# Every second column as the loaded operand of an FFN's products, at chosen distances in SBUF (attention and squared-ReLU FFN in float32, one core)

## The chip, the core and the metric

The kernel runs on one core of a Trainium2 chip. The metric is the device time of one execution in microseconds. A core has a matrix engine (TensorE, PE in the profile), which holds a loaded operand of up to 128 x 128 (LDWEIGHTS, PEld) and streams the columns of a moving operand past it (MATMUL); VectorE (DVE), ScalarE (ACT) and GpSimd (POOL), which work on 128 partitions side by side; and SyncE (SP), whose queue issues the DMAs. SBUF is the working memory, one row of bytes per partition; PSUM takes the products.

## The reference

Eight batches of eight heads, 576 positions, head dimension 64. Each head's output is a sum of two attentions: one on positions averaged by fours and repeated, one on a band of seven positions. Its 4608 tokens of 512 values then go through an FFN:

```python
x = np.ascontiguousarray(attn_out.transpose(0, 2, 1, 3)).reshape(B * S, H * D)
h = x @ w_in                      # 4608 x 512 by 512 x 2048
g = s * (np.maximum(h, 0.0) ** 2) + b
return g @ w_out                  # 2048 x 512
```

## The kernel before

**The FFN.** Tokens go in 18 tiles of 256 (index t), the 2048 columns of w_in in eight pairs of 128 (index p, so one p is 256 columns of w_in and 256 rows of w_out). Each operand is kept as a high and a low part in a rounded format (float32r), and a product is three matmuls: high by high, high by low, low by high. `gemm1(t, p)` forms h transposed: for each of the two column tiles j of the pair and each of four parts k of the 512 values, a 128 x 128 piece of `wi[p]` is the loaded operand and 256 tokens of `xh` or `xl` are the moving one (L544 to L546, 24 matmuls of 256 columns). ACT squares the result, ACT and DVE split it into `gh` and `gl` (or into one tile `gb` for every third p). `gemm2(t, p)` has 128 tokens of `gh` or `gl` as the loaded operand and 512 columns of `wo[p]` as the moving one (L589 to L591, 12 matmuls of 512 columns), and sums over p in PSUM. At p=7 the sum is scaled, the bias is added (L601), and the tile goes out. A step is one `gemm1` and a `gemm2` of some steps before.

**Order.** The list `order` gives the steps: the first three token tiles are mixed over p, then t by t. `advance` lets attention's generators run between steps to a target, so their matmuls and element-wise work stand among the FFN's. Within that, the framework places instructions by its own simulation of time.

**Memory.** All tiles come from three pools: `cst` (constants), `one` (one buffer for each tag) and `two` (two buffers for each tag). They are laid behind one another in the order in which tags are first asked for, so a tile asked for early moves all that come later. `xh` and `xl` of the token tiles other than t=2 have two buffers each, `gh` and `gl` two each, `wi` and `wo` one for each p. For t=2 the tags "os" and "xl2" are borrowed.

In both kernels the five engines' queues hold the same instructions in the same order. What differs is steps and places. Where the operands start, in bytes modulo 256:

```
                              before              after
wi, loaded, p = 2 3 4 5       96                  192
wi, loaded, p = 6             96                  64
wi, loaded, p = 7 0 1         224                 64
xh and xl, moving             32, 32 (2 buffers)  128, 192 (2 buffers)
xh and xl of t=2, moving      96                  192
gh and gl, loaded             32, 32 (2 buffers)  64, 128 (2 buffers)
gb, loaded                    96                  192
wo, moving, p = 2 3 4 5       96                  192
wo, moving, p = 6             96                  64
wo, moving, p = 7 0 1         224                 64
```

Pieces within a tile start at multiples of 512 bytes before; after, the second f tile of a pair starts 4 bytes behind the first.

Of the kernel before, what the change touches and what calls it, by code (L numbers as in the profile page):

```python
# [54 lines left out]

W_MAX = (1.875 - 2.0 ** -23) * 2.0 ** (31 - 127)

OB = {0: (0, 1), 1: (2, 3), 2: (6, 7)}


@with_exitstack
def attention_ffn_kernel(ctx, tc, qk, vw_in, vr_in, vdm, qkn, vn, w_in, w_out, s_in, b_in, out):
# [22 lines left out]

    room = {}

    def make_room(i):
        sc, dg = flat(f"wi{6 - i}", 2048), flat(f"wo{6 - i}", 2048)
        if i == 1:  # L90
            big = flat("x", HP * S, two)
            lp = {"vw": take(big, 0, [P, NG, P]), "vd": take(big, 768, [KM, FAC, P])}
            pl, at = big, 1280
        else:
            big = flat("wi2" if i == 2 else "wo2", 2048)
            pl, at = flat("os" if i == 2 else "xl2", 1024), 512
            lp = {"qk": take(big, 0, [P, 2, SP]), "vw": take(big, 2 * SP, [P, NG, P]),
                  "vd": take(pl, 0, [KM, FAC, P])}
        lp["vr"] = take(sc, 1792, [P, FAC, D])
        return {"sc": sc, "dg": dg, "load": lp, "pl": take(pl, at, [P, 2 * NG, 32]),  # L100
                "sm": take(pl, at + 384, [P, 2, 2 * NG])}
# [26 lines left out]

    mask = cst.tile([P, 3, 32], F32, name="mask")
    nc.gpsimd.memset(mask, 0.0)

    def keep(ap, pattern, base, cm):
# [56 lines left out]
    wi, wo, wst = {}, {}, {}  # L191

    src_i = w_in.bitcast(I32).rearrange("(k c) f -> c k f", c=P)
    src_o = w_out.bitcast(I32).rearrange("(j f) c -> f j c", f=P)

    def load_w(p):

        parts = (("i", src_i[:, :, 512 * p : 512 * p + 512]), ("o", src_o[:, 2 * p : 2 * p + 2]))
        for op, src in parts:
            st = one.tile([P, 1024, 2], I32, tag=f"w{op}{STAGE[p]}", name="wst")  # L200
            nc.sync.dma_start(st.rearrange("p (k f) t -> p k (f t)", k=src.shape[1]), src)
            wst[(p, op)] = st

    def load_quarter(p, op, i):
        if op == "i":
            src = src_i[:, i, 512 * p : 512 * p + 512]
        else:
            src = src_o[:, 2 * p + i // 2, 512 * (i % 2) : 512 * (i % 2) + 512]
        st = two.tile([P, 256, 2], I32, tag="pv", name="wst")
        nc.sync.dma_start(st.rearrange("p f t -> p (f t)"), src)  # L210
        return st
# [21 lines left out]
            nc.vector.tensor_tensor(lo[:, js], f[:, js], hi.bitcast(F32)[:, js], ALU.subtract)  # L233

    def split_w(p):
        with tc.high_priority(offset=-BEHIND.get(p, 0)):
            split_parts(p)

    def split_parts(p):
        wi[p] = one.tile([P, 2, NK, 256], F32R, tag=f"wi{p}", name="wi")  # L240
        wo[p] = one.tile([P, 2, 2, DM], F32R, tag=f"wo{p}", name="wo")
        for op, w in (("i", wi[p]), ("o", wo[p])):
            fl = w.rearrange("p s k f -> p s (k f)")
            if p < len(STAGE):
                st = wst.pop((p, op))
                for j in range(0, 1024, CHUNK[p]):
                    js = slice(j, j + CHUNK[p])
                    convert(st[:, js], fl[:, 0, js], fl[:, 1, js], op, p)
            else:
                for i in range(4):  # L250
                    cs = slice(256 * i, 256 * i + 256)
                    convert(load_quarter(p, op, i), fl[:, 0, cs], fl[:, 1, cs], op, p)
# [80 lines left out]
    def first_unit(b, hp, banks):  # L333
# [71 lines left out]
        try:  # L405
            next(dn)
        except StopIteration as e:
            up = e.value
        ups = tmp([P, SD], "ups")
        nc.scalar.copy(ups, up)  # L410
        yield
        for f in range(2):
# [28 lines left out]
    def local_unit(b, g, banks):  # L441
# [4 lines left out]
        for h in range(2):  # L446
            lqk = one.tile([P, 2 * CH + 2 * HALO, D], F32, tag="big", name="lqk")
            nc.sync.dma_start(lqk, qkn[GROUPS.index((b, g)), h])
            lv = one.tile([P, CH + 2 * HALO, D], F32, tag="vw", name="lv")
            nc.sync.dma_start(lv, vn[GROUPS.index((b, g)), h])  # L450
            ls = take(st[:, h], 0, [P, CH, NO])
            sums = st[:, h, 64 : 64 + CH]
            for o in range(NO):
                pr = two.tile([P, CH, D], F32, tag="pl", name="pr")
                nc.gpsimd.tensor_tensor(  # L455
                    pr, lqk[:, 0:CH], lqk[:, CH + o : 2 * CH + o], ALU.mult)
                nc.vector.tensor_reduce(ls[:, :, o], pr, AX.X, ALU.add)  # L457
                yield
            row = lambda t: t.unsqueeze(2).to_broadcast([P, CH, NO])
            nc.vector.tensor_tensor(ls, ls, omask, ALU.add)  # L460
            lr = two.tile([P, 2, CH], F32, tag="lr", name="lr")
            nc.vector.tensor_reduce(lr[:, 0], ls, AX.X, ALU.max)
            nc.vector.tensor_tensor(ls, ls, row(lr[:, 0]), ALU.subtract)
            nc.scalar.activation(ls, ls, AF.Exp, scale=SCALE)
            nc.vector.tensor_reduce(sums, ls, AX.X, ALU.add)
            nc.vector.tensor_scalar(sums, sums, 1e-9, None, ALU.add)
            nc.vector.reciprocal(lr[:, 1], sums)
            nc.vector.tensor_tensor(ls, ls, row(lr[:, 1]), ALU.mult)
            yield
            for o in range(NO):  # L470
                w = ls[:, :, o : o + 1].to_broadcast([P, CH, D])
                if o == 0:
                    nc.vector.tensor_tensor(acc[:, :, h], lv[:, 0:CH], w, ALU.mult)
                else:
                    pv = two.tile([P, CH, D], F32, tag="pv", name="pv")
                    nc.vector.tensor_tensor(pv, lv[:, o : o + CH], w, ALU.mult)  # L476
                    (nc.vector if o % 3 == 1 else nc.gpsimd).tensor_tensor(  # L477
                        acc[:, :, h], acc[:, :, h], pv, ALU.add)
                yield
# [35 lines left out]
    xs = {}  # L515

    def split_x(t):
        tags = ("os", "xl2") if t == 2 else ("xh", "xl")
        pool = one if t == 2 else two
        xh = pool.tile([P, HP, TB], F32R, tag=tags[0], name="xh")  # L520
        xl = pool.tile([P, HP, TB], F32R, tag=tags[1], name="xl")
        t0 = t * TB
        while t0 < (t + 1) * TB:
            b = t0 // S
            while (b, HP - 1) not in complete:
                next(gen)
            n = min((t + 1) * TB, (b + 1) * S) - t0
            src = xt[b][:, :, t0 - b * S : t0 - b * S + n]
            dst = slice(t0 - t * TB, t0 - t * TB + n)
            nc.scalar.copy(xh[:, :, dst], src)  # L530
            nc.vector.tensor_tensor(
                xl[:, :, dst], src, xh[:, :, dst].bitcast(F32), ALU.subtract)
            t0 += n
        xs[t] = (xh, xl)

    gt = {}
    oacc = {}

    def gemm1(t, p):
        xh, xl = xs[t]  # L540
        ph = bank(6 if t >= 3 and p % 2 else 7 if t == 1 and p < HF else 4, [P, 2, TB], "ph")
        for j, k in itertools.product(range(2), range(NK)):
            f = slice(P * j, P * j + P)
            nc.tensor.matmul(ph[:, j], wi[p][:, 0, k, f], xh[:, k], start=(k == 0), stop=False)  # L544
            nc.tensor.matmul(ph[:, j], wi[p][:, 0, k, f], xl[:, k], start=False, stop=False)  # L545
            nc.tensor.matmul(ph[:, j], wi[p][:, 1, k, f], xh[:, k], start=False, stop=(k == NK - 1))  # L546
# [1 line left out]
            both = one.tile([P, 2, 2, TB], F32R, tag="xl2", name="gb")  # L548
            gh, gl = both[:, 0], both[:, 1]
        else:  # L550
            gh = two.tile([P, 2, TB], F32R, tag="gh", name="gh")
            gl = two.tile([P, 2, TB], F32R, tag="gl", name="gl")
        with tc.high_priority():
            nc.scalar.activation(ph, ph, AF.Relu)  # L554
            nc.scalar.activation(ph, ph, AF.Square)  # L555
# [18 lines left out]
    def gemm2(t, p):  # L574
# [5 lines left out]
            oacc[t] = [bank(i, [P, DM], "po") for i in ob]  # L580
        po = oacc[t]
        end = t == NB - 1 and p == NFP - 1
        os_ = one.tile([P, 2, DM], F32, tag="os", name="os") if p == NFP - 1 else None
        for m in range(2):
            ms = slice(P * m, P * m + P)
            for j in range(2):
                first = p == 0 and j == 0
                last = p == NFP - 1 and j == 1
# [1 line left out]
                nc.tensor.matmul(po[m], gh[:, j, ms], wo[p][:, 1, j], start=False, stop=False)  # L590
                nc.tensor.matmul(po[m], gl[:, j, ms], wo[p][:, 0, j], start=False, stop=last)  # L591
            if end:
                r0 = TB * t + P * m
                for c in (0, DM // 2):
                    cs = slice(c, c + DM // 2)
                    nc.vector.scalar_tensor_tensor(
                        os_[:, m, cs], po[m][:, cs], sb_s, bias[:, cs], ALU.mult, ALU.add)
                    nc.sync.dma_start(out[r0 : r0 + P, cs], os_[:, m, cs])
        if p == NFP - 1 and not end:
            for m in range(2):  # L600
                nc.vector.scalar_tensor_tensor(  # L601
                    os_[:, m], po[m], sb_s, bias, ALU.mult, ALU.add)
            nc.sync.dma_start(
                out[TB * t : TB * t + TB, :].rearrange("(m p) c -> p m c", p=P), os_)


    units = [(b, hp) for b in range(B) for hp in range(HP)]
# [10 lines left out]
    for hp in range(2, HP):  # L618
        load_pair(0, hp)
    load_w(0)  # L620
    sb_s = cst.tile([P, 1], F32, name="sb_s")
    nc.sync.dma_start(sb_s, bass.AP(s_in.tensor, s_in.offset, [[0, P], [1, 1]]))
    sb_b = cst.tile([P, 1], F32, name="sb_b")
    nc.sync.dma_start(sb_b, bass.AP(b_in.tensor, b_in.offset, [[0, P], [1, 1]]))
    clear(1)
    bk = banks(0, 1, 2, 3, 5, 6, 7)
# [7 lines left out]
    split_w(0)  # L634
    load_w(1)
    load_w(2)
    split_x(0)
    split_x(1)


# [117 lines left out]
```

## Time and profile before

| | |
|---|---|
| time, median of 3 runs | 975.49 us (lowest 974.06) |
| profiled execution: time, span | 974.94 us, 973.1 us |
| TensorE busy | 937.4 us, 96% of the span |
| VectorE, ScalarE, GpSimd busy | 646.8, 478.8, 425.0 us |
| mean granted TensorE clock | 0.982 |

The span is from the first to the last instruction. A line such as `L544 PE MATMUL ph<-xh,wi 128*128 128x256 f32` is line 544's matmul on TensorE into the tile ph from xh (moving) and wi (loaded), 128 rows by 128 loaded columns, 256 moving columns. Matmuls overlap one another, so a busy time is not a rate; the distance from one start to the next is.

### The profile page before, as it was taken

The page shows a single profiled execution, that of the slowest core. Times are in us where ns is not written, and L with a number is a line of the kernel's source. Part 1 is how long each engine was busy: PE and PEld are TensorE (multiplying, and loading weights), DVE is VectorE, ACT ScalarE, POOL GpSimd, SP SyncE. Part 2 cuts the span into 40 slices and gives each one's busy share as a digit, 9 for nine tenths or more (in the row PEclk, how much of TensorE's full clock was granted, in tenths as well). Part 3 has the DMA queues.
Part 4 walks back from the last instruction along what each step waited for, and adds up shares of the span by engine and source line. Part 5 has one row for each costly group of instructions (what it writes and reads, how often), then busy time and mean ns, then how long its engine had stood idle before and what let it go on. Part 6 is the DMA issues. An engine that isn't in the chain of part 4 may idle for free.

```text
span 973.1 us, 18535 instructions
## 1 busy us (share of the span) xinstructions
PE 937.4 (96%) x7316; PEld 840.0 (86%) x7316; DVE 646.8 (66%) x1175; ACT 478.8 (49%) x1141; POOL 425.0 (44%) x455
## 2 busy tenths in 40 slices
PE   5769999999999999999999999999999999999998
PEld 4558888788999989889989898999899999998997
DVE  5999985864468778878787975876787772211121
ACT  5878775453755454534545344454454444333231
POOL 9422011100167686776767585575776750000000
PEclk9579999999999999999999999999999999999999
DMA  9746422102233232322323232231323100000000
GB/s 314 261 132 204 166 65 73 60 31 86 88 122 112 86 101 85 133 65 72 106 93 102 80 98 80 78 112 58 112 90 111 55 23 1 23 1 22 1 23 22
DMA packets 32103, 86.26 MB, mean 89 GB/s; under 512 B 3344, under 2 KB 7952, under 8 KB 32016
## 3 DMA queue, kind: packets, MB, share of 16 engines
q1 hardware_dynamic: 32016, 85.08, 26.4%
q8 instruction: 57, 0.93, 0.4%
q14 instruction: 30, 0.25, 0.1%
HBM read 75.63 MB, written 9.44 MB: 87 GB/s over the span
## 4 chain that ended last, share of the span: by engine, by line
PE 76%; DVE 7%; POOL 6%; DMA 6%; issue 3%; ACT 2%; DVEq 0%; SPq 0%; POOLq 0%; ACTq 0%
PE ph L544 12%; PE ph L545 12%; PE ph L546 12%; PE po L589 11%; PE po L590 11%; PE po L591 11%; DMA tqk<-in_qk_dram 3%; POOL pr L455 2%; PE sa L297 2%; DMA lqk<-in_qkn_dram 1%; POOL acc L477 1%; DMA wst<-in_moe_w_out_dram 1%; PE up L328 1%; PE ol L420 1%; PE ot L486 1%
## 5 line engine op out<-in xcount | busy, mean ns | idle before, releaser
L544 PE MATMUL ph<-xh,wi 128*128 128x256 f32 x1152 | 327.2, 284 | 5.3 <-DVE gl L557 2.5
L545 PE MATMUL ph<-xl,wi 128*128 128x256 f32 x1152 | 324.0, 281 | 0.0
L546 PE MATMUL ph<-xh,wi 128*128 128x256 f32 x1152 | 323.6, 281 | 0.0
L455 POOL TENSOR_TENSOR pr<-lqk 128x576 f32<-128x576 f32 x140 | 203.0, 1473 | 90.1 <-DMA lqk<-in_qkn_dram 53.9
L544 PEld LDWEIGHTS ph<-xh,wi 128*128 128x128 f32 x1152 | 217.1, 188 | 12.8 <-DVE gl L557 3.4
L545 PEld LDWEIGHTS ph<-xl,wi 128*128 128x128 f32 x1152 | 217.0, 188 | 5.0 <-issue 0.2
L546 PEld LDWEIGHTS ph<-xh,wi 128*128 128x128 f32 x1152 | 217.3, 189 | 0.1
L554 ACT ACTIVATE ph<-ph 128x512 f32<-128x512 f32 x144 | 83.7, 581 | 236.7 <-PE ph L546 236.5
L589 PE MATMUL po<-wo,gh 128*128 128x512 f32 x456 | 183.0, 402 | 0.2 <-ACT gh L556 0.2
L590 PE MATMUL po<-wo,gh 128*128 128x512 f32 x456 | 181.5, 398 | 0.0
L591 PE MATMUL po<-wo,gl 128*128 128x512 f32 x456 | 179.5, 399 | 0.0
L557 DVE TENSOR_TENSOR gl<-ph,gh 128x512 fp32r<-128x512 f32 x114 | 77.9, 683 | 110.9 <-ACT gh L556 110.5
L477 POOL TENSOR_TENSOR acc<-acc,pv 128x576 f32<-128x576 f32 x80 | 114.6, 1433 | 68.0 <-DVE acc L477 33.5
L457 DVE TENSOR_REDUCE st<-pr 128x9 f32<-128x576 f32 x140 | 105.9, 756 | 40.9 <-POOL pr L455 38.8
L287 POOL TENSOR_TENSOR dq<-vq 64x64 f32<-64x64 f32 x58 | 25.6, 441 | 192.4 <-PE up L326 190.2
L556 ACT CAST gh<-ph 128x512 fp32r<-128x512 f32 x114 | 66.8, 586 | 70.6 <-PE po L590 68.5
L591 PEld LDWEIGHTS po<-wo,gl 128*128 128x128 f32 x456 | 85.7, 188 | 17.3 <-issue 0.2
L476 DVE TENSOR_TENSOR pv<-lv,st 128x576 f32<-128x576 f32 x120 | 87.2, 747 | 20.2 <-POOL acc L477 19.6
L589 PEld LDWEIGHTS po<-wo,gh 128*128 128x128 f32 x456 | 85.7, 188 | 15.8 <-ACT gh L556 0.8
L590 PEld LDWEIGHTS po<-wo,gh 128*128 128x128 f32 x456 | 85.8, 188 | 15.6
L555 ACT ACTIVATE ph<-ph 128x512 f32<-128x512 f32 x144 | 83.8, 582 | 3.4
L590 PE MATMUL po<-wo,gb 128*128 128x512 f32 x120 | 48.2, 402 | 0.0
(145 smaller groups left out, 1261.1 us busy)
## 6 DMA issues: line engine op xcount, KB each, us to landing
tqk<-in_qk_dram SPq DMA_DIRECT2D x30, 584.0 KB, 4.0
lqk<-in_qkn_dram SPq DMA_DIRECT2D x20, 768.0 KB, 4.4
lv<-in_vn_dram SPq DMA_DIRECT2D x20, 480.0 KB, 3.5
out_dram<-os SPq DMA_DIRECT2D x17, 512.0 KB, 3.0
wst<-in_moe_w_in_dram SPq DMA_DIRECT2D x7, 1024.0 KB, 5.5
wst<-in_moe_w_out_dram SPq DMA_DIRECT2D x7, 1024.0 KB, 5.3
tvd<-in_vdm_dram SPq DMA_DIRECT2D x29, 160.0 KB, 2.7
tvr<-in_vr_dram SPq DMA_DIRECT2D x29, 128.0 KB, 2.1
```

Source lines behind the costliest of these rows:

```text
L455: nc.gpsimd.tensor_tensor(pr, lqk[:, 0:CH], lqk[:, CH + o : 2 * CH + o], ALU.mult)
L457: nc.vector.tensor_reduce(ls[:, :, o], pr, AX.X, ALU.add)
L476: nc.vector.tensor_tensor(pv, lv[:, o : o + CH], w, ALU.mult)
L477: (nc.vector if o % 3 == 1 else nc.gpsimd).tensor_tensor(acc[:, :, h], acc[:, :, h], pv, ALU.add)
L544: nc.tensor.matmul(ph[:, j], wi[p][:, 0, k, f], xh[:, k], start=(k == 0), stop=False)
L545: nc.tensor.matmul(ph[:, j], wi[p][:, 0, k, f], xl[:, k], start=False, stop=False)
L546: nc.tensor.matmul(ph[:, j], wi[p][:, 1, k, f], xh[:, k], start=False, stop=(k == NK - 1))
L554: nc.scalar.activation(ph, ph, AF.Relu)
L555: nc.scalar.activation(ph, ph, AF.Square)
L589: nc.tensor.matmul(po[m], gh[:, j, ms], wo[p][:, 0, j], start=first, stop=False)
L590: nc.tensor.matmul(po[m], gh[:, j, ms], wo[p][:, 1, j], start=False, stop=False)
L591: nc.tensor.matmul(po[m], gl[:, j, ms], wo[p][:, 0, j], start=False, stop=last)
```

## The change

The loaded operand of both products becomes every second column of the same memory: in `gemm1` the two f tiles of a pair are its even and its odd columns, in `gemm2` the two token tiles are the even and the odd tokens. So that the products stay the same, w_out's rows are loaded in the same alternation, and the output's rows are written so. Empty tiles (`skip`) of 128, 192 and 64 bytes and 16 unused elements at the end of each x buffer set where operands start. To make room and to set the start of all, the mask takes a buffer of the tag "pv", `ups` that of `ptm`, `sb_s` and `sb_b` one tile, and `xh` and `xl` lie in one tile.

```diff
+SKIP = (0, 128, 192, 0, 0, 0, 64, 0, 0)
...
+    def skip(n, pool=one):
+        if n:
+            pool.tile([P, n // 4], F32, tag=f"skip{next(skips)}", name="skip")
...
-    mask = cst.tile([P, 3, 32], F32, name="mask")
+    mask = two.tile([P, 3, 32], F32, tag="pv", name="mask")
...
-    src_o = w_out.bitcast(I32).rearrange("(j f) c -> f j c", f=P)
+    src_o = w_out.bitcast(I32).rearrange("(q f j) c -> f q j c", f=P, j=2)
...
+        if p == 0:
+            skip(SKIP[1])
...
     def split_w(p):
+        if p == 0:
+            skip(SKIP[2])
...
     def split_parts(p):
+        if p == 1:
+            for h in range(2):
+                one.tile([P, 2, CH], F32, tag=f"lr{h}", name="lr")
+            skip(SKIP[-1])
...
-        ups = tmp([P, SD], "ups")
+        ups = tmp([P, SD], "ups") if alt else one.tile([P, SD], F32, tag="ptm", name="ups")
...
-            lr = two.tile([P, 2, CH], F32, tag="lr", name="lr")
+            lr = one.tile([P, 2, CH], F32, tag=f"lr{h}", name="lr")
...
-        xh = pool.tile([P, HP, TB], F32R, tag=tags[0], name="xh")
-        xl = pool.tile([P, HP, TB], F32R, tag=tags[1], name="xl")
+        if t == 2:
+            xh, xl = (pool.tile([P, HP * TB], F32R, tag=g, name="x2") for g in tags)
+        else:
+            both = pool.tile([P, 2 * HP * TB + 16], F32R, tag="xhl", name="xhl")
+            xh, xl = both[:, 0 : HP * TB], both[:, HP * TB : 2 * HP * TB]
+        xh, xl = (v.rearrange("p (k c) -> p k c", k=HP) for v in (xh, xl))
...
-            f = slice(P * j, P * j + P)
+            f = slice(j, 256, 2)
...
-            gh = two.tile([P, 2, TB], F32R, tag="gh", name="gh")
-            gl = two.tile([P, 2, TB], F32R, tag="gl", name="gl")
+            i = next(gs)
+            if i < 2:
+                skip(SKIP[4 + 2 * i])
+            gh = one.tile([P, 2, TB], F32R, tag=f"gh{i % 2}", name="gh")
+            if i < 2:
+                skip(SKIP[5 + 2 * i])
+            gl = one.tile([P, 2, TB], F32R, tag=f"gl{i % 2}", name="gl")
...
+        rows = out[TB * t : TB * t + TB, :].rearrange("(p m) c -> p m c", m=2)
...
-            ms = slice(P * m, P * m + P)
+            ms = slice(m, TB, 2)
...
-                    nc.sync.dma_start(out[r0 : r0 + P, cs], os_[:, m, cs])
+                    nc.sync.dma_start(rows[:, m, cs], os_[:, m, cs])
...
-    sb_s = cst.tile([P, 1], F32, name="sb_s")
+    sb = cst.tile([P, 2], F32, name="sb")
+    sb_s, sb_b = sb[:, 0:1], sb[:, 1:2]
```

More of the change, by code (lines that the diff above doesn't have):

```diff
@@ L86, in attention_ffn_kernel @@
     room = {}
+    def skip(n, pool=one):
+        if n:
+            pool.tile([P, n // 4], F32, tag=f"skip{next(skips)}", name="skip")
+    skips = itertools.count()
     def make_room(i):
+        if i == 1:
+            skip(SKIP[0])
         sc, dg = flat(f"wi{6 - i}", 2048), flat(f"wo{6 - i}", 2048)
@@ L193, in attention_ffn_kernel @@
     src_i = w_in.bitcast(I32).rearrange("(k c) f -> c k f", c=P)
-    src_o = w_out.bitcast(I32).rearrange("(j f) c -> f j c", f=P)
+    src_o = w_out.bitcast(I32).rearrange("(q f j) c -> f q j c", f=P, j=2)
     def load_w(p):
-        parts = (("i", src_i[:, :, 512 * p : 512 * p + 512]), ("o", src_o[:, 2 * p : 2 * p + 2]))
+        parts = (("i", src_i[:, :, 512 * p : 512 * p + 512]), ("o", src_o[:, p]))
+        if p == 0:
+            skip(SKIP[1])
         for op, src in parts:
@@ L207, in load_quarter @@
         else:
-            src = src_o[:, 2 * p + i // 2, 512 * (i % 2) : 512 * (i % 2) + 512]
+            src = src_o[:, p, i // 2, 512 * (i % 2) : 512 * (i % 2) + 512]
         st = two.tile([P, 256, 2], I32, tag="pv", name="wst")
@@ L517, in split_x @@
     def split_x(t):
-        tags = ("os", "xl2") if t == 2 else ("xh", "xl")
+        tags = ("os", "xl2")
         pool = one if t == 2 else two
-        xh = pool.tile([P, HP, TB], F32R, tag=tags[0], name="xh")
-        xl = pool.tile([P, HP, TB], F32R, tag=tags[1], name="xl")
+        if t == 2:
[4 more added lines that the diff above has]
+        xh, xl = (v.rearrange("p (k c) -> p k c", k=HP) for v in (xh, xl))
         t0 = t * TB
@@ L536, in attention_ffn_kernel @@
     gt = {}
+    gs = itertools.count()
     oacc = {}
@@ L592, in gemm2 @@
             if end:
-                r0 = TB * t + P * m
                 for c in (0, DM // 2):
@@ L602, in gemm2 @@
                     os_[:, m], po[m], sb_s, bias, ALU.mult, ALU.add)
-            nc.sync.dma_start(
-                out[TB * t : TB * t + TB, :].rearrange("(m p) c -> p m c", p=P), os_)
+            nc.sync.dma_start(rows, os_)
     units = [(b, hp) for b in range(B) for hp in range(HP)]
@@ L620, in attention_ffn_kernel @@
     load_w(0)
-    sb_s = cst.tile([P, 1], F32, name="sb_s")
+    sb = cst.tile([P, 2], F32, name="sb")
+    sb_s, sb_b = sb[:, 0:1], sb[:, 1:2]
     nc.sync.dma_start(sb_s, bass.AP(s_in.tensor, s_in.offset, [[0, P], [1, 1]]))
-    sb_b = cst.tile([P, 1], F32, name="sb_b")
     nc.sync.dma_start(sb_b, bass.AP(b_in.tensor, b_in.offset, [[0, P], [1, 1]]))
@@ L636, in attention_ffn_kernel @@
     load_w(2)
+    skip(SKIP[3], two)
     split_x(0)
```

## The prediction

> **What bounds the kernel now.** I read the shares of the engines first, then the stretches of time, then who TensorE waited for, and last the starts of single matmuls. The page:
>
> ```profile
> PE 937.4 (96%) x7316; PEld 840.0 (86%) x7316; DVE 646.8 (66%) x1175; ACT 478.8 (49%) x1141; POOL 425.0 (44%) x455
> PE 76%; DVE 7%; POOL 6%; DMA 6%; issue 3%; ACT 2%; DVEq 0%; SPq 0%; POOLq 0%; ACTq 0%
> ```
>
> By stretches (us, then each engine's busy time and count, the granted TensorE clock, the DMA share, GB/s):
>
> ```profile
> 20.00:60.00 40.00, 27.23 (x441) 22.20 (x441) 35.83 (x87) 33.05 (x96) 18.02 (x27) 0.70 0.69 237
> 60.00:100.00 40.00, 35.75 (x365) 32.10 (x364) 39.56 (x71) 32.00 (x62) 7.50 (x10) 0.87 0.56 188
> 100.00:970.00 870.00, 864.51 (x6298) 777.61 (x6297) 559.12 (x995) 405.13 (x957) 381.52 (x368) 1.00 0.22 72
> 820.00:920.00 100.00, 100.00 (x650) 90.75 (x649) 17.72 (x24) 33.26 (x57) 0.00 (x0) 1.00 0.03 11
> ```
>
> From 100 to 970 us TensorE is busy for 864.5 of 870 us at a granted clock of 1.00. Behind 820 us nobody else has much to do and it is still full. So the kernel is TensorE's stream of matmuls, and the time is their number times the distance from one start to the next. The longest waits of TensorE are few and early (us in total, times, longest):
>
> ```profile
> PE sa L297 <- ACT dq L277: 7.3, 1, 7.3
> PE ol L420 <- ACT db L403: 4.6, 2, 2.7
> PE ph L544 <- DVE gl L557: 2.5, 3, 1.2
> ```
>
> A busy time hides the distance, since matmuls overlap. It has to be read from starts (start us, duration us). One step of the FFN is 24 matmuls of 256 columns (L544 to L546) and 12 of 512 (L589 to L591). First the first product at two f pairs p, then the second product at two places:
>
> ```profile
> 886.12 0.28 PE L544 MATMUL ph<-xh,wi 128*128 128x256 f32 x1
> 886.36 0.28 PE L546 MATMUL ph<-xh,wi 128*128 128x256 f32 x1
> ...
> 888.74 0.28 PE L546 MATMUL ph<-xh,wi 128*128 128x256 f32 x1
> ...
> 866.58 0.28 PE L544 MATMUL ph<-xh,wi 128*128 128x256 f32 x1
> ...
> 869.29 0.28 PE L546 MATMUL ph<-xh,wi 128*128 128x256 f32 x1
> ...
> 517.26 0.39 PE L589 MATMUL po<-wo,gb 128*128 128x512 f32 x1
> ...
> 519.30 0.28 PE L544 MATMUL ph<-xh,wi 128*128 128x256 f32 x1
> ...
> 495.60 0.39 PE L591 MATMUL po<-wo,gl 128*128 128x512 f32 x1
> ...
> 496.30 0.40 PE L591 MATMUL po<-wo,gl 128*128 128x512 f32 x1
> ```
>
> The same instruction runs at two speeds. At p=2 (886 us) the last 22 of a group of 24 start (888.74 - 886.36) / 21 = **113.3 ns** apart. At p=7 (866 us) a group of 24 takes (869.29 - 866.58) / 23 = **117.8 ns** each. In the second product nine distances from 517.26 to 519.30 give **226.7 ns**, and three from 495.60 to 496.30 give 233 ns. In the late part every group at p = 2 to 5 is of the fast kind and every one at p = 6, 7, 0, 1 of the slow kind, for one token tile after another, while clock and instruction stay the same. Only the tiles' places in SBUF differ by p. At t=2, where x stands elsewhere, it is slower still, (209.80 - 207.04) / 23 = **120.0 ns**:
>
> ```profile
> 207.04 0.28 PE L544 MATMUL ph<-xh,wi 128*128 128x256 f32 x1
> ...
> 209.80 0.28 PE L546 MATMUL ph<-xh,wi 128*128 128x256 f32 x1
> ```
>
> So something that hangs on addresses costs up to 4.5 or 6.7 ns a matmul. It is this that a change of steps and distances can touch.
>
> **What the change touches.** The five queues hold the same instructions in the same order as before; only names, steps, addresses and the semaphores of three waits differ. So nothing is counted anew. The terms are rates.
>
> How much there is to gain follows from one token tile, that is eight steps:
>
> ```profile
> 841.72 0.28 PE L544 MATMUL ph<-xh,wi 128*128 128x256 f32 x1
> ...
> 886.12 0.28 PE L544 MATMUL ph<-xh,wi 128*128 128x256 f32 x1
> ...
> 930.52 0.28 PE L544 MATMUL ph<-xh,wi 128*128 128x256 f32 x1
> ```
>
> From p=2 to p=2 it is 44.40 us, twice. With all its matmuls at the fast rows it would be 8 x (24 x 113.3 + 12 x 226.7) ns = 43.51 us. The address-dependent part is 0.89 us, times 18 token tiles **16.0 us**. Earlier tiles have more of it (t=2), and stretches in which attention's matmuls stand between have waits that stay; I leave both out.
>
> What the stride does to a load: no loaded operand of this kernel has a step now, so its price is bounded by rows. Loads of 32, 64, 96 and 128 columns from 120 us on (mean ns):
>
> ```profile
> L377 PEld LDWEIGHTS sl<-tqk 64*32 64x32 f32 x480 | 5.6, 107 | 2.4 <-issue 1.3
> L420 PEld LDWEIGHTS ol<-db,tvw 128*64 128x64 f32 x144 | 6.3, 136 | 2.2 <-issue 1.3 <-ACT ups L410 0.4
> L297 PEld LDWEIGHTS sa<-kd,dq 128*96 128x96 f32 x150 | 21.6, 162 | 3.4
> L545 PEld LDWEIGHTS ph<-xl,wi 128*128 128x128 f32 x1080 | 203.2, 188 | 4.4
> 886.37 0.19 PEld L544 LDWEIGHTS ph<-xh,wi 128*128 128x128 f32 x1
> ```
>
> That is (188 - 107) / 96 = 0.84 ns a column, so a load reads for about 108 ns behind a fixed 80 ns. It starts 10 ns or less behind the matmul before (886.37 against 886.36) and runs beside that matmul's columns. From this follow two things. In 108 ns a load with step one passes 512 bytes of its row, while 256 moving columns pass 1024 bytes in 113.3 ns: the moving operand overtakes the load. With step two the load passes 1024 bytes too. The two then run **in step**, and how far apart they are stays as the addresses set it, which is what the distances in memory would be good for. Second, in the first product 108 of 113.3 ns are filled by the load, so a load that reads over 5% slower becomes the bound there; in the second product (226.7) it could double for nothing. Lower end: the whole 16.0 us go. Upper end: loads at double price, 216 ns, put (216 - 116) x 3456 matmuls = 346 us on top. I take the lower one, since the load has as many columns as before and the kernel's rows price columns alone.
>
> [...] No run here has shown a stepped load yet.
>
> The rest I cost at nothing. The mask lies in one of the two "pv" buffers; the next user of it stands behind the mask's last reader (L149, 0.4 us) on DVE anyway. "ups" shares a buffer with "ptm": the next copy L319 on ACT must now find L423 done, which is two 0.45 us operations of DVE, nine times, 8 us of ACT if nothing hid it; ACT is busy 405 of 870 us and TensorE has other matmuls queued. "gh", "gl", "lr" and "xh" with "xl" keep two buffers each. The w_out loads and the outputs move the same bytes in longer runs; the last output was 1.7 us to landing and stays on the end.
>
> **Rivals.** *Below the fast rows.* Even 113.3 and 226.7 may hold a loss: both are 0.443 ns a column. The column sums' matmul, which streams 512 fp32 columns twice, shows another price:
>
> ```profile
> L571 PE MATMUL cs<-bias,ones 128*128 128x512 f32 x2 | 1.0, 592 | 0.0
> 230.62 1.02 PE L571 MATMUL cs<-bias,ones 128*128 128x512 f32 x2
> ```
>
> Two passes end 1.02 us behind the first start, each lasting 0.592, so they start 0.428 us apart, 0.836 ns a column. If the FFN's columns go at twice that rate, 0.418 ns, 256 take 107 ns and 512 take 214: another 24 x 6.3 + 12 x 12.7 = 304 ns a step, 43.7 us in 144 steps. For it: a loss of a sixteenth proportional to bytes looks like memory, and the moving operands, which start 32 bytes behind a multiple of 64 now, start on one afterwards. Against it: none of the groups that I read runs below the fast rows, whatever its distance, and the loss is as large in the second half of 512 columns, when the load (108 ns) is over. All of it gives 916 us, half 938, two thirds 930. [...]
>
> *Nothing changes.* The fast and slow groups may come from something that stays, such as the order in which groups follow one another, and one row speaks for it: the matmul at 496.30 has a next start 1.6 us later, so no load beside it, and still lasts 0.40 us like its neighbours beside loads. Then the time is 975, give or take 5. [...]
>
> *In step and in the same place.* The two streams that run in step meet for the whole load where their distance is a bad one. By the distances, modulo 256 bytes, the eight w_in tiles now stand at 64 or 192 from the first x buffer but at 0 or 128 from the second, and t=2 before, which was also at 0 or 128, is the 120.0 ns row. Its price for a tile: 8 x (24 x 120.0 + 12 x 236) = 45.70 us (236 = 233 + 3, the same addition), 1.30 more than now. On all 18 tiles 23 us, 998; on the half that use the second buffer 12 us, 987. It decides from the point where the mean distance of the first product passes the present (113.3 + 117.8) / 2 = 115.6 ns.
>
> **How the numbers follow.** The profiled execution has a span of 973.1 and a time of 974.94; the median of the runs is 975.49, so 0.55 goes on top. Forecast: 975.49 - 16.0 = **959.5**. Its own range is 953 to 967. Chances: forecast 0.38; below the fast rows 0.32 (916 to 950); nothing changes 0.17 (970 to 980); in the same place, or load-bound, 0.13 (985 and up). What a measurement of this kernel can tell from no change is about 2%, 19.5 us: below 956 counts as faster, above 995 as slower. Of the forecast's 0.38 some 0.07 lies below 956, so faster 0.39; of the last case 0.08 lies above 995; the rest, 0.53, is within. The range leaves out the full loss of a sixteenth (some 0.08) and the last case's upper part (0.10): 920 to 982.
>
> **What would show it.** Right: L544's starts 113 to 114 ns apart at every p, none at 118 or 120; loads still near 188 ns; TensorE still 99% busy from 100 to 970 us; a token tile of 43.5 us. Below the fast rows: starts near 107 to 110 and 214 to 217. Nothing changed: the same pattern by p. The same place: groups that alternate by token tile, since x does. Load-bound: loads well above 188 ns and the first product's distance with them, the second's not. I would be wrong altogether if attention's chain, which has DVE and POOL pieces, took over once TensorE is faster; it would show as idle time ahead of L544.

## The result, and the profile after

The changed kernel takes **989.65 us** (median of 4 runs, 987.04 to 992.35) against 975.76 us of the kernel before: ratio 1.0148, 95% interval 1.0107 to 1.019. One of the four runs of the kernel before took 3223 us and is left out of the ratio; the other three have a median of 975.49. The changed kernel is slower by one and a half per cent, where 959.5 us were forecast, and outside the range of 920 to 982. The difference is below the 2% that this kernel's measurement was said to tell, but the interval is clear of no change.

The page of the changed kernel (span 986.3 us, before 973.1), first the engines' busy time, then two groups of loads (behind the bar: busy us, mean ns of one, idle time before it):

```profile
PE 951.9 (97%) x7316; PEld 864.4 (88%) x7316; DVE 648.0 (66%) x1175; ACT 479.3 (49%) x1141; POOL 422.6 (43%) x455
L570 PEld LDWEIGHTS ph<-xhl,wi 128*128 128x128 f32 x1088 | 213.5, 196 | 8.5 <-ACT xhl L555 3.0
L621 PEld LDWEIGHTS po<-wo,gh 128*128 128x128 f32 x456 | 89.0, 195 | 14.6 <-ACT gh L587 1.6
```

TensorE's busy time grew by 14.5 us, the span by 13.2; VectorE, ScalarE and GpSimd stand within 2.4 us of before. The records of both products' loads went from 188 ns to 196 and 195. By stretches:

```profile
100.00:970.00 870.00, 866.98 (x6265) 792.20 (x6265) 558.48 (x992) 404.48 (x955) 380.35 (x368) 1.00 0.22 72
820.00:920.00 100.00, 100.00 (x641) 92.13 (x640) 18.65 (x28) 32.48 (x55) 0.00 (x0) 1.00 0.03 11
```

The clock is 1.00 and TensorE full, as before: from 820 to 920 us it holds 641 matmuls where it held 650. So it is still the stream of matmuls that bounds, and the stream is slower. From 100 to 970 us TensorE idles 3.0 us against 5.5; a slower stream waits for the others less.

The distances from start to start, in the timeline. One group of the first product at w_in tile p=3 with nine matmuls of the second ahead of it, and the starts of p=2 two token tiles apart (line numbers moved: L544 to L546 are now L570 to L572, L589 to L591 are L621 to L623):

```profile
900.15 0.40 PE L621 MATMUL po<-wo,gh 128*128 128x512 f32 x1
...
902.25 0.28 PE L570 MATMUL ph<-xhl,wi 128*128 128x256 f32 x1
...
905.02 0.28 PE L572 MATMUL ph<-xhl,wi 128*128 128x256 f32 x1
...
851.90 0.28 PE L570 MATMUL ph<-xhl,wi 128*128 128x256 f32 x1
...
942.68 0.28 PE L570 MATMUL ph<-xhl,wi 128*128 128x256 f32 x1
```

The first product runs at (905.02 - 902.25) / 23 = **120.4 ns**, at t=2 (210.60 to 213.38 us) at 120.9; the second at (902.25 - 900.15) / 9 = 233 ns. There is no group of the fast kind (113.3 ns) left: every group of 20 or more matmuls of the first product from 100 us on has a mean of 119.6 to 121.6 ns, whatever its w_in tile and x buffer. A token tile takes (942.68 - 851.90) / 2 = 45.39 us instead of 44.40.

Below, "first" and "second" are the means of the distances between neighbouring starts of one product from 100 us on (some 3034 and 1400 of them in each trace). Some 72 and 60 longer ones, over 150 and 280 ns, are left out; their sums are alike in all traces (15 to 17 and 19 to 22 us). Before: **116.39 and 231.22 ns**. After: **120.28 and 232.41**. With 3456 and 1728 matmuls that is 13.4 + 2.1 = 15.5 us more, less the 2.5 us of idle time: 13.0, against 13.2 in the span.

### The profile page after: what moved, and what is told of

Same layout as the page of the kernel before. It is cut to its first block, busy times and chain, and to the rows that moved or that the text cites. A ratio compares the mean times of both kernels' runs of the same rounds, so it can differ in the third digit from the quotient of the medians.

```text
span 986.3 us, 18535 instructions
## 1 busy us (share of the span) xinstructions
PE 951.9 (97%) x7316; PEld 864.4 (88%) x7316; DVE 648.0 (66%) x1175; ACT 479.3 (49%) x1141; POOL 422.6 (43%) x455
## 4 chain that ended last, share of the span: by engine, by line
PE 88%; DMA 5%; DVE 4%; ACT 2%; issue 1%; SPq 0%; POOL 0%; DVEq 0%; ACTq 0%; POOLq 0%
PE ph L570 14%; PE ph L571 14%; PE ph L572 14%; PE po L621 13%; PE po L622 13%; PE po L623 13%; DMA wst<-in_moe_w_out_dram 2%; PE sa L317 2%; DMA tqk<-in_qk_dram 1%; PE up L348 1%; PE ot L506 1%; PE ol L440 1%; DMA flat<-in_vr_dram 1%; PE sl L397 1%; PE tp L335 1%; PE tr L337 1%
## 5 line engine op out<-in xcount | busy, mean ns | idle before, releaser
L570 PE MATMUL ph<-xhl,wi 128*128 128x256 f32 x1088 | 313.2, 288 | 2.9 <-ACT xhl L555 2.7
L571 PE MATMUL ph<-xhl,wi 128*128 128x256 f32 x1088 | 310.9, 286 | 0.0
L572 PE MATMUL ph<-xhl,wi 128*128 128x256 f32 x1088 | 310.2, 285 | 0.0
L570 PEld LDWEIGHTS ph<-xhl,wi 128*128 128x128 f32 x1088 | 213.5, 196 | 8.5 <-ACT xhl L555 3.0
L571 PEld LDWEIGHTS ph<-xhl,wi 128*128 128x128 f32 x1088 | 213.2, 196 | 4.1 <-issue 0.2
L572 PEld LDWEIGHTS ph<-xhl,wi 128*128 128x128 f32 x1088 | 213.4, 196 | 0.0
L621 PE MATMUL po<-wo,gh 128*128 128x512 f32 x456 | 183.2, 402 | 1.0 <-ACT gh L587 1.0
L623 PE MATMUL po<-wo,gl 128*128 128x512 f32 x456 | 179.5, 399 | 0.0
L588 DVE TENSOR_TENSOR gl<-ph,gh 128x512 fp32r<-128x512 f32 x114 | 77.9, 684 | 121.0 <-ACT gh L587 120.9
L623 PEld LDWEIGHTS po<-wo,gl 128*128 128x128 f32 x456 | 88.7, 195 | 15.1 <-issue 0.2
L621 PEld LDWEIGHTS po<-wo,gh 128*128 128x128 f32 x456 | 89.0, 195 | 14.6 <-ACT gh L587 1.6
L622 PEld LDWEIGHTS po<-wo,gh 128*128 128x128 f32 x456 | 88.9, 195 | 13.3
L496 DVE TENSOR_TENSOR pv<-lv,st 128x576 f32<-128x576 f32 x120 | 87.2, 747 | 14.5 <-POOL acc L497 13.8
```

Source lines behind the costliest of these rows:

```text
L621: nc.tensor.matmul(po[m], gh[:, j, ms], wo[p][:, 0, j], start=first, stop=False)
```

## The experiments

### One step at a time

Three kernels have the changed kernel's places and differ in which operand is stepped. Contiguous in both products:

```diff
-    src_o = w_out.bitcast(I32).rearrange("(q f j) c -> f q j c", f=P, j=2)
+    src_o = w_out.bitcast(I32).rearrange("(q j f) c -> f q j c", f=P, j=2)
...
-            f = slice(j, 256, 2)
+            f = slice(P * j, P * j + P)
...
-        rows = out[TB * t : TB * t + TB, :].rearrange("(p m) c -> p m c", m=2)
+        rows = out[TB * t : TB * t + TB, :].rearrange("(m p) c -> p m c", m=2)
...
-            ms = slice(m, TB, 2)
+            ms = slice(P * m, P * m + P)
```

> The changed kernel with both loaded operands contiguous again (f tiles and token tiles as before, w_out's rows and the output's rows too), all distances and moved tiles kept. Theory A, the step makes a load read longer and that sets the pace of the first product: loads back at 188 ns, 971 to 978 us. Theory B, the new places are the cost and the step is free: still 986 to 992. Theory C, two streams in step meet at bad distances: without the step they are not in step, so 971 to 978 as well.

Measured: 979.88 us against 973.98, ratio 1.0059 (1.0038 to 1.0079). First 117.95 ns, second 231.12. This is 2 us above the range of A and C and 6 us below B's. So the places alone already cost 0.6%, and taking the steps away gives back the rest.

The step in w_in's loads alone (the last two edits of that diff):

> The changed kernel with the step only in w_in's loads; g's loads contiguous. A: nearly the whole loss stays, since the first product has only some 5 ns between a load's 108 ns and the distance of 113.3: 985 to 990, first product 120 ns, second 231. B: 986 to 992. C: 980 to 990, with the spacing alternating by token tile.

Measured: 988.96 us, ratio 1.0151 (1.0126 to 1.0175). First 120.34 ns, second 230.97.

The step in g's loads alone (the first two edits):

> The changed kernel with the step only in g's loads; w_in's loads contiguous. A: the second product has 226 ns for a load of 116, so nothing of the loss: 972 to 979, loads of g at 195, second product within 1.5 ns of before. B: 986 to 992. C: a part of the loss, 978 to 984.

Measured: 980.18 us, ratio 1.0071 (1.0048 to 1.0094). First 117.89 ns, second 232.27.

The pages' groups of loads, of the contiguous kernel, of w_in's step and of g's step, in this order:

```profile
L570 PEld LDWEIGHTS ph<-xhl,wi 128*128 128x128 f32 x1088 | 206.1, 189 | 9.0 <-ACT xhl L555 2.7
```

```profile
L570 PEld LDWEIGHTS ph<-xhl,wi 128*128 128x128 f32 x1088 | 213.3, 196 | 9.7 <-ACT xhl L555 2.7
L621 PEld LDWEIGHTS po<-wo,gh 128*128 128x128 f32 x456 | 85.7, 188 | 16.6 <-ACT gh L587 1.8
```

```profile
L570 PEld LDWEIGHTS ph<-xhl,wi 128*128 128x128 f32 x1088 | 205.8, 189 | 10.4 <-ACT xhl L555 2.6
L621 PEld LDWEIGHTS po<-wo,gh 128*128 128x128 f32 x456 | 88.9, 195 | 13.5 <-ACT gh L587 0.5
```

The records follow the step, each in its own product: 188 or 189 ns without it, 195 or 196 with it. In the first product 7 ns more of a load's record cost 9 us (988.96 against 979.88), as A had it. In the second product the step costs nothing beyond the uncertainty here (980.18 against 979.88); its rate rises by 1.2 ns, 2 us by the sum below. That 512 columns simply hide the load is not shown by this, as the next experiment tells.

### The load by itself

A kernel without attention and FFN runs groups of 64 matmuls. A name says the moving columns (small 128, half 256, full 512), the step of the loaded operand and the distance in bytes of loaded from moving operand, modulo 256 (a 0, c 64, e 128, g 192). With 128 moving columns the matmul is short (another can start 58 to 62 ns behind it, as the second such kernel shows below) and the load sets the pace (111.8 ns and more):

```diff
+for i in range(COUNT):
+    lo = LOAD0 + (d + off) // 4 + 1024 * (i % 8)
+    mo = MOVE0 + off // 4 + 512 * (i % 8 + 1)
+    w = big[:, lo : lo + 128 * step]
+    w = w[:, 0 : 128 * step : step] if step > 1 else w
+    nc.tensor.matmul(po, w, big[:, mo : mo + n], start=i == 0, stop=i == COUNT - 1)
```

> No attention and no FFN: 33 groups of 64 matmuls on float32r data in SBUF, in each group one moving width (128, 256, 512), one step of the loaded operand (1, 2, 3, 4, 8) and one distance (0, 64, 128, 192 bytes modulo 256, at two alignments); the output is one tile's copy, not the reference's. With 128 moving columns the load alone sets the pace. A: 128 columns, step 1 108 ns from start to start, step 2 115 to 117, step 4 and 8 longer by as much again or more, whatever the distance; 256 columns, step 2 at 118 to 122 at every distance; 512 columns the same for steps 1 and 2. B: step 1 and 2 alike, spread over distances of 5 ns or more. C: at step 2 and 256 columns a spread of 5 ns or more between distances, at step 1 hardly any.

Its timeline (start, duration of the group, operation, count) and the stretches of the first two groups:

```profile
25.82 7.03 PE L65 MATMUL small_one_a<-big 128*128 128x128 f32 x61 [0.16 <-ACT big L52]
32.69 7.35 PE L65 MATMUL small_two_a<-big 128*128 128x128 f32 x61
39.87 12.89 PE L65 MATMUL small_three_a<-big 128*128 128x128 f32 x63
...
119.94 7.70 PE L65 MATMUL half_one_c<-big 128*128 128x256 f32 x64
127.48 7.75 PE L65 MATMUL half_one_e<-big 128*128 128x256 f32 x64
...
142.62 7.84 PE L65 MATMUL half_two_a<-big 128*128 128x256 f32 x64
150.29 7.84 PE L65 MATMUL half_two_c<-big 128*128 128x256 f32 x64
157.97 7.84 PE L65 MATMUL half_two_e<-big 128*128 128x256 f32 x64
165.65 7.85 PE L65 MATMUL half_two_g<-big 128*128 128x256 f32 x64
...
203.89 15.09 PE L65 MATMUL half_four_a<-big 128*128 128x256 f32 x64
218.82 14.69 PE L65 MATMUL full_one_a<-big 128*128 128x512 f32 x64
233.35 15.09 PE L65 MATMUL full_one_c<-big 128*128 128x512 f32 x64
248.28 15.04 PE L65 MATMUL full_one_e<-big 128*128 128x512 f32 x64
...
277.82 15.10 PE L65 MATMUL full_two_a<-big 128*128 128x512 f32 x64
292.75 14.88 PE L65 MATMUL full_two_c<-big 128*128 128x512 f32 x64
307.47 14.98 PE L65 MATMUL full_two_e<-big 128*128 128x512 f32 x64
```

```profile
25.90:32.60 6.70, 6.70 (x61) 6.70 (x61) 0.00 (x0) 3.38 (x1) 0.00 (x0) 1.00 0.01 2
32.80:39.80 7.00, 7.00 (x62) 7.00 (x61) 0.29 (x1) 0.00 (x0) 0.00 (x0) 1.00 0.00 0
```

At clock 1.00 a load with step two repeats every (39.87 - 32.69) / 61 = **117.7 ns**. The contiguous group gives (32.69 - 25.82) / 61 = 112.6 ns, but it stands behind an idle time, and its first distance of 165 ns belongs to that; the other 60 have a mean of **111.8 ns**. With 256 columns a group of step two takes (150.29 - 142.62) / 64 = 119.8 ns, and 120.0 from half_two_c to half_two_e and from there to half_two_g: **the same at distances 0, 64 and 128**. The contiguous group at 64 takes (127.48 - 119.94) / 64 = 117.8. With 128 columns the clock fell within the group at step three (granted 0.63 from 39.9 to 52.5 us, 0.50 from 52.6 on), so steps beyond two were measured again at full clock (below). With 256 columns and step four a matmul takes (218.82 - 203.89) / 64 = 233.3 ns, nearly twice the contiguous 117.8, and a load with step four alone takes 234 (below): at that step the load sets the distance from matmul to matmul.

With 512 columns A expected steps one and two to be alike, and that missed. Contiguous loads take 227.0 ns at distance 0 and 233.3 at 64, loads with step two 233.3 at 0 and 230.0 at 64. So the step is not hidden there: it adds 6.3 ns at distance 0 and takes off 3.3 at 64. The kernel with g's step alone shows the same in smaller numbers. Its second product goes from 230.0 to 232.8 ns at distance 0 and from 232.8 to 230.8 at 64, against the contiguous kernel, and in the mixture of distances most of it cancels.

### The distances under the step

The changed kernel with its steps, without its distances:

```diff
-SKIP = (0, 128, 192, 0, 0, 0, 64, 0, 0)
+SKIP = (0, 0, 0, 0, 0, 0, 0, 0, 0)
...
-            both = pool.tile([P, 2 * HP * TB + 16], F32R, tag="xhl", name="xhl")
+            both = pool.tile([P, 2 * HP * TB], F32R, tag="xhl", name="xhl")
```

> The steps of the changed kernel are kept and its chosen distances are taken out: the empty tiles and the 16 unused elements behind each x buffer are gone. If the stepped load itself bounds the first product (a load with step two alone repeats every 117.7 ns), distances have nothing to give there: the first product stays at 119.5 to 121 ns, the time within 985 to 993 us, ratio 1.011 to 1.018. If the distances still matter under the step, the mean of the first product moves by more than 1 ns and the time by more than 3.5 us against the changed kernel's 989.65.

Measured: 988.97 us against 975.12, ratio 1.0151 (1.0135 to 1.0168). First 120.16 ns, second 231.98. In its timeline, at 904 us:

```profile
904.00 0.28 PE L570 MATMUL ph<-xhl,wi 128*128 128x256 f32 x1
...
906.76 0.28 PE L572 MATMUL ph<-xhl,wi 128*128 128x256 f32 x1
```

That is 2.76 / 23 = 120.0 ns. The w_in tiles now stand at 192 (six) or 0 (two) from both x buffers, no longer at 64 or 192 from one and 0 or 128 from the other, and neither the first product nor the time moved: under the step the distances do nothing for the first product. The step without the chosen distances costs the whole 13.9 us, so the 5.9 us of the places and the 9 us of the step are not two terms that add. What each is worth depends on which is taken away first. No run has these places with contiguous loads.

### The distances without the step

The contiguous kernel of the first experiment put the eight w_in tiles at 0 or 128 from the second x buffer, because the 16 unused elements at the end of each x buffer move the second one. Without them both x buffers start at 128:

```diff
-            both = pool.tile([P, 2 * HP * TB + 16], F32R, tag="xhl", name="xhl")
+            both = pool.tile([P, 2 * HP * TB], F32R, tag="xhl", name="xhl")
```

> Contiguous loads with the changed kernel's places, as before in the run with both loads contiguous, but without the 16 unused elements that end each x buffer. Both x buffers then start at 128 modulo 256 bytes, and every w_in tile stands 64 or 192 bytes from them; none is at 0. If the loss of 0.6% that the contiguous kernel showed is that of the tiles at distance 0 (119.5 ns), the first product comes back from 117.95 to about 116.4 ns, the time to 973 to 977 us, ratio 0.997 to 1.003. If the loss has another cause (moved tiles, DMA shapes), it stays at 979 to 981 us.

Measured: 975.02 us against 975.12, ratio 1.0008 (0.9992 to 1.0023). First 116.78 ns, second 231.08. The 0.6% came back, so it was these distances and not the moved tiles. The DMAs have the same shapes in both runs. In the contiguous kernel's trace the groups of w_in tile p=2 at distance 0 are the visible part of it, (890.15 - 887.40) / 23 = 119.6 ns:

```profile
887.40 0.28 PE L570 MATMUL ph<-xhl,wi 128*128 128x256 f32 x1
...
890.15 0.28 PE L572 MATMUL ph<-xhl,wi 128*128 128x256 f32 x1
```

Contiguous loads with all w_in and w_out tiles, gh, gl and gb at 192 and x at 128, so 64 in the first product and 0 in the second:

```diff
-SKIP = (0, 128, 192, 0, 0, 0, 64, 0, 0)
+SKIP = (0, 0, 192, 64, 0, 0, 0, 0, 64)
```

> Contiguous loads, and places chosen by what the runs showed so far: all w_in and w_out tiles, gh, gl and gb start at 192, both x buffers at 128 modulo 256 bytes. The first product's distance is 64 everywhere but at t=2 (fast kind, 113.3 to 114.5 ns where the matmuls stand back to back), the second's is 0 (227 ns). If the distance alone sets the rate: 3456 matmuls by about 2 ns and 1728 by about 3.5 ns less than before, that is 7 to 13 us, 962 to 969 us, ratio 0.987 to 0.993. If something else than the distance made p=6 slow before (it stood at 64 too), only part comes: 970 to 975 us.

Measured: 973.36 us against 975.12, ratio 0.998 (0.9965 to 0.9994). First 117.10 ns, second 228.41. The second product became what was expected, (904.04 - 902.00) / 9 = 226.7 ns; the first did not, (901.88 - 899.17) / 23 = 117.8 at the distance of 64:

```profile
899.17 0.28 PE L570 MATMUL ph<-xhl,wi 128*128 128x256 f32 x1
...
901.88 0.28 PE L572 MATMUL ph<-xhl,wi 128*128 128x256 f32 x1
902.00 0.39 PE L621 MATMUL po<-wo,gb 128*128 128x512 f32 x1
...
904.04 0.28 PE L570 MATMUL ph<-xhl,wi 128*128 128x256 f32 x1
```

The distance alone therefore doesn't make a group of the first product fast.

### The load by itself, at a held clock

A second kernel without attention and FFN has the FFN's order of pieces. Its small groups of 24 matmuls stand each behind 24 matmuls of 512 columns ("keep"), which are to hold the clock (granted 1.00 from 225 to 230 us and from 258.1 to 263.5, and 0.76 to 0.81 in the three that stand behind a small group of step three or four and ahead of another). "da" to "dh" are distances of 0, 32, ... 224 bytes, "l" to "p" five places of the loaded operand.

> Attention and FFN are left out; TensorE runs groups of matmuls alone, in the FFN's order of pieces. Groups of 128 columns at steps 1 to 4, each right behind 24 matmuls of 512 columns that keep the clock up, show the load's own period: if the load is what a step slows, 112.6 ns at step one, 117.7 at two, clearly longer at three and four, wherever the load stands. Groups of 256 columns at step one: by the distance theory 113 to 118 ns at 64 bytes and near 120 at 0, at every one of the five places of the load; if the place itself matters, the five differ at one distance. Groups of 256 at step two: 120 ns at each of four distances. Groups of 512: 227 ns at 0, 233 at 64.

```profile
33.54 5.91 PE L64 MATMUL half_da<-big 128*128 128x256 f32 x48
39.29 5.84 PE L64 MATMUL half_db<-big 128*128 128x256 f32 x48
44.97 5.82 PE L64 MATMUL half_dc<-big 128*128 128x256 f32 x48
50.63 5.79 PE L64 MATMUL half_dd<-big 128*128 128x256 f32 x48
...
230.65 2.79 PE L64 MATMUL small_one_l<-big 128*128 128x128 f32 x24
233.28 5.71 PE L64 MATMUL full_keep_one_h<-big 128*128 128x512 f32 x24
...
247.01 2.93 PE L64 MATMUL small_two_l<-big 128*128 128x128 f32 x24
249.78 5.68 PE L64 MATMUL full_keep_two_h<-big 128*128 128x512 f32 x24
...
263.60 4.22 PE L64 MATMUL small_three_l<-big 128*128 128x128 f32 x24
267.66 7.27 PE L64 MATMUL full_keep_three_h<-big 128*128 128x512 f32 x24
...
285.71 5.60 PE L64 MATMUL small_four_l<-big 128*128 128x128 f32 x24
291.15 7.30 PE L64 MATMUL full_keep_four_h<-big 128*128 128x512 f32 x24
```

```profile
263.70:267.60 3.90, 3.90 (x25) 3.90 (x24) 0.69 (x1) 0.00 (x0) 0.00 (x0) 1.00 0.00 0
285.80:291.10 5.30, 5.30 (x25) 5.30 (x24) 0.69 (x1) 0.00 (x0) 0.00 (x0) 1.00 0.01 3
```

From a small group's start to the next group's it is 2.63, 2.77, 4.06 and 5.44 us at steps 1, 2, 3 and 4, at clock 1.00. In each of these groups the second matmul starts only 58 to 62 ns behind the first; so 128 columns take no longer than that, and it is the load that sets the pace of the others. The other 23 distances have means of **111.8, 117.8, 174 and 234 ns**: step two costs 6 ns a load, step three 62 and step four 122. At steps 1 and 2 the second place of the load gives the same; at steps 3 and 4 the clock fell there (0.91 and 0.85). With 256 contiguous columns distance 0 gives 5.75 us for 48, 119.8 ns, and 64 gives 117.9; with 512, 0 gives 227.7 and 64 gives 233.3, as in the first kernel. The five places of the loaded operand differ by nothing (119.8 to 120.0 at distance 0, 117.7 to 117.9 at 64). No group of 256 columns here was of the fast kind at any of eight distances: the lowest of their means is 117.3 ns. With 256 columns at step two, the groups at distances 64 and 128 read 120 and 121 ns; the clock fell in the one at 0 (0.68).

### How a group is entered

Here "fast" is a group's mean near 114 ns, "slow" one near 118. In the kernel before, a first product at distance 64 right behind a second product was fast in 26 of 29 groups where the last load also stood at 64, and in 5 of 16 where it stood at 0. If the entry decided, this was worth giving up the second product's 227 ns: gh, gl and gb at 0, so that both products stand at 64 (edits against the kernel with chosen distances; not shown are gb, which is moved by 16 elements within its tile, and an empty tile of 192 bytes behind the second gl):

```diff
-SKIP = (0, 0, 192, 64, 0, 0, 0, 0, 64)
+SKIP = (0, 0, 192, 64, 64, 0, 0, 0, 64)
```

> Contiguous loads; as the run with places chosen by distance, but gh, gl and gb start at 0 modulo 256 bytes, 64 behind w_out's tiles, so the second product stands at distance 64 (slow kind, 233 ns) and the first at 64. In the runs so far a first product at distance 64 was of the fast kind (113.3 ns) nearly only behind a second product whose last load also stood at 64 (before: 26 of 29 groups), and of the slow kind behind one at 0 (with places chosen by distance: 69 of 72). If how the stream enters a group decides between its two speeds: first product near 114.5 ns, second 232 to 233, 3456 by 2 to 2.5 ns less than before and 1728 by 1.5 more, some 5 us less than before, 968 to 972 us, ratio 0.993 to 0.997. If the entry does not decide, the first product stays at 117 and the time goes to 977 to 981.

Measured: 976.95 us against 974.68, ratio 1.0027 (1.0014 to 1.004). First 116.18 ns, second 232.99. The expectation missed: of the groups at distance 64 right behind a second product only 28 of 73 were fast. With the last load at 0, in the kernel with chosen distances, only 3 of 72 were. So the last load's distance matters, but is not the rule of the entry.

The same with gh at distance 0 and only gl at 64 (the main edit; not shown is gb's low part, moved by 16 elements):

```diff
+            for half in ("hl" if i % 2 == 0 else "lh"):
+                if (i, half) in ((0, "l"), (1, "h")):
+                    skip(64 if i == 0 else 192)
+                v = one.tile([P, 2, TB], F32R, tag=f"g{half}{i % 2}", name=f"g{half}")
+                gh, gl = (v, gl) if half == "h" else (gh, v)
```

> As the run with both products at distance 64, but gh stands at distance 0 from w_out's tiles and gl alone at 64; gl is the loaded operand of the last matmul of each second product. If that last load sets the entry and the two gh products of every three keep the second product's speed: first product near 114.5 ns, second 229 to 231, 6 to 11 us less than before, 964 to 969 us. If the change between two distances within the second product costs it its fast kind, 233 and 968 to 972; if it takes the entry away too, 975 to 980.

Measured: 972.98 us against 974.68, ratio 0.9975 (0.9961 to 0.9988). First 115.27 ns, second 231.15. 59 of 72 such groups were fast, and from 790 us on all of them:

```profile
882.32 0.28 PE L571 MATMUL ph<-xhl,wi 128*128 128x256 f32 x1
...
884.94 0.28 PE L573 MATMUL ph<-xhl,wi 128*128 128x256 f32 x1
885.06 0.39 PE L622 MATMUL po<-wo,gh 128*128 128x512 f32 x1
...
887.14 0.28 PE L571 MATMUL ph<-xhl,wi 128*128 128x256 f32 x1
```

(884.94 - 882.32) / 23 = 113.9 ns, and in the second product (887.14 - 885.06) / 9 = 231 ns. This is the lowest time here, a quarter of a per cent below the kernel before; it stays above the time that was expected at best, and the second product lost its fast kind (228.41 to 231.15 ns) as the first gained it.

The traces hold one more sign. In these last two kernels the distance from the last start of the second product to the first start of the first product tells the two kinds apart: it is 232 ns or more ahead of nearly all groups near 114 ns and 231 or less ahead of nearly all near 118. In the kernel before, with the last load at 64, it is the other way round (228 to 231 ns ahead of the 26 groups near 114, 232 to 236 ahead of the three near 118). So the moment of entry goes with the kind, but no run shows a rule for it.

### The sum of the rates

Each run's change of time by its two mean distances alone, (first - 116.39) x 3456 + (second - 231.22) x 1728, beside the difference of the medians measured (for the changed kernel against 975.49):

| kernel | first, ns | second, ns | by the rates, us | measured, us |
|---|---|---|---|---|
| changed kernel | 120.28 | 232.41 | +15.5 | +14.2 |
| contiguous, same places | 117.95 | 231.12 | +5.2 | +5.9 |
| step in w_in alone | 120.34 | 230.97 | +13.2 | +15.0 |
| step in g alone | 117.89 | 232.27 | +7.0 | +6.2 |
| steps, no distances | 120.16 | 231.98 | +14.3 | +13.9 |
| contiguous, no pad | 116.78 | 231.08 | +1.1 | -0.1 |
| distances 64 and 0 | 117.10 | 228.41 | -2.4 | -1.8 |
| both at 64 | 116.18 | 232.99 | +2.3 | +2.3 |
| gl alone at 64 | 115.27 | 231.15 | -4.0 | -1.7 |

Two rates explain every run within 2.3 us. Nothing else of the change has a price that shows beyond that.

## Why the prediction was wrong

**What bounds the kernel** was right: TensorE's stream sets the time, in every run, and start distances are the quantity to read. **The terms are rates** was right too, and so was costing the moved tiles, the buffers and the semaphores at nothing (contiguous without the pad: ratio 1.0008) and the outputs' DMAs (with g's step: 980.18 against 979.88). The w_out loads in longer runs came only together with w_in's step, where the rates leave 1.8 us unexplained.

**The step that failed is the price of the stepped load**: "I take the lower one, since the load has as many columns as before and the kernel's rows price columns alone." A contiguous load says nothing on a step. The load alone went from 111.8 to 117.7 ns, and with it the first product from a mean of 116.39 to 120.28 ns: a loss where the prediction had a gain. The prediction's own upper end, loads at double price, is what step four shows (234 ns).

**The slack was mis-sized as well.** The prediction had 108 of 113.3 ns filled and the load as the bound only if it "reads over 5% slower". That 108 came from the slope of load records over columns, with 80 ns taken as a fixed part that overlaps. The measured period is 111.8, so 1.5 ns was free instead of 5.3, and the load became 5.3% slower. The fast rows of 113.3 were already near the load's own pace. For the second product the prediction had a load that "could double for nothing". With the step in g alone no cost shows in the time, but at a fixed distance it does show: 227.0 to 233.3 ns at 0, and 230.0 at 64 where contiguous has 233.3. That the two nearly cancel here is luck of the distances.

**The gain of 16.0 us had no source.** The in-step argument wanted the chosen distances to take the slow kinds away. Under the step they do nothing for the first product (988.97 us without them, 989.65 with them), and the step takes away the fast kind that the kernel before had in 45 of its 113 groups of 20 or more matmuls. Without the step the distances matter, but not in the way that I read from p: the tiles of p = 5 and p = 6 both stood at 64 before, and the one ran fast, the other slow. In the kernel before all groups of the fast kind but three stand at distance 64 (the three at 192, with means of 113.3 to 114.0 ns), and yet it does not bring that kind by itself (117.8 ns at 64 in the kernel with chosen distances).

**The rivals.** *In the same place, or load-bound*, held to be 0.13 likely, is what happened, at the place named (the mean of the first product passed 115.6 ns, to 120.28) and between its two prices (987 and 998). That the price fits is luck: it came from distance 0, and the cause was the other half of its name. (Its 236 ns adds 3 ns where the rows give 2.2, which is 1.4 us of the price.) Its sign, groups that alternate with the x buffer, is weak: the buffers' groups differ by at most 2 ns. *Below the fast rows* is refuted for the first product, since a contiguous load alone repeats every 111.8 ns and the rival needed 107; the second had no group below 226.6. *Nothing changes* is refuted by the contiguous kernel, where places alone cost 0.6%. With matmuls and loads alone in a group, too, distance 0 or 64 makes 227.7 or 233.3 ns.

**The signs.** Of those named for a load-bound product, the first product's distance (120) and the loads' records (196) came in the trace; that the second product's rate stayed was nearly right (+1.2 ns).

**What stays open.** Why a first product with stepped loads takes 120.0 ns when the load alone takes 117.7 (that the load grows with the step, and at step four sets the pace, is shown; the 2.3 ns in between at step two are not explained); what puts a contiguous group at distance 64 into its fast or its slow kind (the distance of the last load before it is not it); and so whether a layout exists with 113.3 and 226.7 ns at once. Its worth, by the sum above, would be some 18 us.

## What to carry to other kernels

Before a load's cost is called hidden, measure its period with nothing else to bound it; a slack read from overlapping records was 5.3 ns on paper and 1.5 on the chip. Changing the step of an operand that feeds the busiest engine can cost even where its columns stay the same: here 6 ns a load cost 9 us in the product with 256 moving columns. In the one with 512 the time did not move clear of the noise, and there the step took at some distances what it gave back at others; measure such a product at each distance before calling the step free. When two changes come together, a step and its distances, run them apart first: here one of the two undid whatever the other could have given.

## What the hardware showed

**The price of a step.** At clock 1.00 the load alone takes 111.8 ns contiguous, and 117.8, 174 and 234 ns at steps 2, 3 and 4: step two adds 6 ns, and each of the next two steps 56 to 60. In the first kernel's groups at half clock (0.50) a load with step four takes (67.48 - 52.56) / 64 = 233 ns, so as long as at full clock, and one with step eight 240; steps one and two take (96.50 - 82.84) / 64 = 213.4 and (110.15 - 96.50) / 64 = 213.3. So the period at step four did not follow the granted clock, while those at steps one and two nearly doubled and came out alike. At step two and clock 1.00 the load is 5.3% slower than contiguous (117.7 against 111.8 ns), and the first product, whose fast groups at 113.3 ns left it 1.5, shows it: with the step in w_in alone its mean went from 117.95 to 120.34 ns.

**The places of two operands in SBUF change a matmul's pace.** With contiguous loads the same instruction had 113.3, 117.8 or 119.8 ns (256 columns) and 227 or 233 ns (512), and distances of the loaded from the moving operand modulo 256 bytes go with it. The two products want different ones: 64 is where the first has its fast kind (113.3 ns, before at p=2), while the second has it at 0 (227.0 ns) and is slow at 64 (233.3). A step in the loaded operand turns the second's order round (233.3 at 0, 230.0 at 64). That two groups at the same distance can run at two paces, each held to the group's end, was not expected: in the kernel before, the second halves of the first product's uninterrupted groups of 20 or more at 64 run at 113.3 to 113.4 ns or at 117.7 to 117.8.
